# Attention and two MLPs on one core: the first MLP's last 1024 tokens in two blocks of 512

## The chip, the cores and the metric

The kernel runs on one core of a Trainium2 chip. The metric is the device time of one execution in microseconds (us): the median of the runs, with the lowest and the highest beside it.

## What is computed

Three stages follow one another: an attention over 4 batches of 8 heads with 576 tokens, a gated MLP on the 2304 tokens that come out of it, and a second MLP with two up projections. Cut to what matters here:

```python
x = attention(q, k, v, tau)          # 2304 tokens x 512
h = x @ w_in                         # 512 -> 2048
y = (h * sigmoid(h)) @ w_out         # 2048 -> 512
a, b = y @ w_a, y @ w_b              # 512 -> 1536 each
out = (a * b) @ w_o2                 # 1536 -> 512
```

All inputs are float32. Each operand of the MLPs' matmuls is split into a high part in the reduced format float32r and a low part (the rest), and each product is made of three matmuls: high by high, low weight by high, high weight by low.

## The kernel before

**Tiling.** Tokens lie along the columns of the matmuls in the first MLP. It works in 9 blocks of 256 tokens (`TB`, index `j`). A block has 16 slices of 128 features (index `f`); a slice with its block is a unit. The up part of a unit (`mlp1_up`) is 12 matmuls, three for each of four pieces of x, and fills one PSUM bank, `hb` or, from the fifth block on for every second unit, `hc`. The gate follows: tanh on ScalarE (line 713), `(tanh + 1) * h` on VectorE (line 716), the cast to the high part `gh` on ScalarE (line 719), the low part `gl` on VectorE (line 722). The down part (`mlp1_down`) is 12 matmuls of 256 columns that add the slice to y, which lies in two banks: `sb`, or `sd` for every second block after attention. On TensorE the up part of a unit stands ahead of the down part of the unit before it. At a block's end y is halved into `yo` by ScalarE and VectorE and stored to DRAM. x comes from DRAM as well, is cast on ScalarE (line 676) and subtracted on GpSimd (line 679).

The second MLP works in blocks of 512 tokens and 12 slices of 128 features. `mlp2_up` makes a and b (12 matmuls each, line 833), `mlp2_down` four groups of three matmuls (line 877), one for each 128 tokens, in four banks. Its input is loaded from DRAM and split by `load_y` (cast on line 807, subtraction on line 810).

**Weights.** Each of the 32 weight tiles of the first MLP and the 36 of the second is loaded as raw words and rebuilt in several steps (`split_weight`): `wt` on ScalarE (line 314), three VectorE operations (lines 321 to 330), a sum on GpSimd (line 334), the cast of the high part on ScalarE (line 338), and the low part on GpSimd or VectorE (line 342). The second MLP's weights take the places of the first's (ring `w`, 32) as its last block gives them up; the first four have places of their own (ring `w2`) from the end of attention on.

**Order.** Nothing is scheduled by the compiler. The class `Plan` lists tasks with an engine, a cost, a rank and the tasks they come after, and it holds rings: a taker of a ring waits until the one that many places before it has been freed. `run` plays the tasks through in modelled time, and this order is the order of the instructions on every engine and of the transfers on SP's queue. Each engine runs its instructions in that order. `closed` marks the end of attention, when its memory is given to others, and `closed1` the end of the first MLP.

Of the kernel before, what the change touches and what calls it, by code (L numbers as in the profile page):

```python
# [12 lines left out]
F32 = mybir.dt.float32  # L13
# [8 lines left out]
P = 128  # L22
# [10 lines left out]
NB = NT // TB  # L33
# [173 lines left out]
def fused_kernel(ctx: ExitStack, tc: tile.TileContext, qk, qk2, v, tau, w_in, w_out, w_a, w_b, w_o2, out):  # L207
# [19 lines left out]
    def pool(stack, name, bufs, side="left", **kw):  # L227
# [4 lines left out]
    p1, att = ExitStack(), ExitStack()  # L232
# [17 lines left out]
    ps_1 = pool(p1, "ps_1", 1, space=PSUM)  # L250
    ap = {n: pool(att, n, RINGS[n]) for n in ("qk", "v", "t", "e", "pa", "pb")}
# [206 lines left out]
    def softmax(parts, total):  # L458
# [10 lines left out]
        def scores():  # L469
            s["s"] = (ps_1 if bank == "sb" else ps_s).tile([P, 2, 512], F32, name=bank)  # L470
# [189 lines left out]
    up_last, down_last, y_dma = [None], [None], []  # L660

    def load_x(j):
        s = xs[j] = {}

        def split(c):
            need = [t for (b, half, heads), ts in x_dma.items() for t in ts
                    if heads == c and b * S + HALVES[half][0] < (j + 1) * TB and b * S + sum(HALVES[half]) > j * TB]

            def load():
                s["r", c] = xb_p.tile([P, TB], F32, name="xr", bufs=RINGS["xr"])  # L670
                nc.sync.dma_start(out=s["r", c], in_=xT_d[c, :, j * TB:(j + 1) * TB])

            def hi():
                s["h", c] = xb_p.tile([P, TB], F32R, name="xh")
                s["l", c] = xb_p.tile([P, TB], F32R, name="xl")
                nc.scalar.copy(out=s["h", c], in_=s["r", c])
# [4 lines left out]
            ld = dma(-1, P * 4 * TB, load, after=need, take=["xr"], slack=SLACK)  # L681
            h = pl.add("ACT", act_ns(TB), R_AUX, hi, [ld], ["xb"])
            l = pl.add("Pool", pool_ns(TB), R_AUX, lo, [h])
            pl.free("xr", l)
# [5 lines left out]
    def mlp1_up(n, j, f):  # L690
# [3 lines left out]
        bank = "hc" if n >= TWO_H and n % 2 else "hb"  # L694

        def up(c):
            def fn():
                if c == 0:
                    s["h"] = (pools["hc"] if bank == "hc" else ps_1).tile([P, 512], F32, name=bank)[:, :TB]
# [25 lines left out]
        for c in range(NC):  # L725
            p = pl.add("PE", 3 * pe_ns(TB), R, up(c),
# [4 lines left out]
            if f == NF - 1:  # L731
                pl.free("xb", p)
        th = pl.add("ACT", act_ns(TB, True), R_AUX, tanh, [p], ["g", "th"])
        ga = pl.add("DVE", dve_ns(TB), R_AUX, gate, [th])
        pl.free(bank, ga)
        hh = pl.add("ACT", act_ns(TB), R_AUX, hi, [ga])
        ll = pl.add("DVE", dve_ns(TB), R_AUX, lo, [hh], port=True)
        pl.free("th", ll)
        g_ready[j, f] = (hh, ll)

    def mlp1_down(n, j, f):


        ring = "sd" if j * NF >= TWO_H and j % 2 == 0 else "sb"
        prods = [(e, a, "gh") for e in range(NC) for a in (1, 0)] + [(e, 0, "gl") for e in range(NC)]

        def down(k0):
            def fn():
                if f == 0 and k0 == 0:
                    ys[j] = (pools["hc"] if ring == "sd" else ps_1).tile([P, 2, 512], F32, name=ring).rearrange("p k (e t) -> p (k e) t", e=2)  # L750
# [9 lines left out]
        for k0 in (0, 4, 8):  # L760
            p = pl.add("PE", 4 * pe_ns(TB), R, down(k0), [g_ready[j, f][k0 == 8], *w_ready["out", f]],
                       [ring] if f == 0 and k0 == 0 else [], behind=[down_last[0]])
# [243 lines left out]
```

## Time and profile before

| what | value |
|---|---|
| median of 3 runs | 1191.71 us |
| lowest and highest | 1190.04 and 1193.56 us |
| the profiled execution's own time | 1190.77 us |
| its span | 1189.0 us |
| TensorE's matmuls busy | 1154.5 us (97%) |
| weight loads on TensorE, beside them | 994.4 us (84%) |
| VectorE, ScalarE, GpSimd busy | 646.2, 543.9, 255.2 us |

A profile is of one execution. A busy time is what an engine's instructions took, one after another; matmuls overlap, so their single durations are longer than the distance from one to the next, and the distance is what a stream of them costs. An idle time before an instruction is given to the one that ended it. A wait for a transfer counts from the engine's side. Names such as `hb<-xh,w` mean that the tile `hb` is written from `xh` and `w`.

### The profile page before, as it was taken

The numbers are of one execution on the slowest core, as the hardware profiler recorded it, in microseconds if no ns is written. First come the engines' busy times: TensorE is split into PE (matmuls) and PEld (weight loads), VectorE is DVE, ScalarE is ACT, GpSimd is POOL, SyncE is SP. The second block draws the span as 40 slices with busy tenths as digits, with TensorE's granted clock in tenths as the row PEclk, the third lists the DMA queues.
The fourth block names the chain that finished last, engine by engine and source line by source line (L and its number), as shares of the span: only waits on it lengthen the run. The fifth ranks groups of instructions, "written<-read, shape, count | busy, mean of one in ns | idle before, by whom it ended". The sixth has DMA issues, their size and how long they took to land.

```text
span 1189.0 us, 19705 instructions
## 1 busy us (share of the span) xinstructions
PE 1154.5 (97%) x7675; PEld 994.4 (84%) x7675; DVE 646.2 (54%) x1448; ACT 543.9 (46%) x1071; POOL 255.2 (21%) x212
## 2 busy tenths in 40 slices
PE   8879999999999999989999999999999999999998
PEld 6556667898898888989999999877888888888898
DVE  7989897777777877473233257775211311211121
ACT  7777786666666766553233245443211211211121
POOL 3655554222111311131000034553000000000000
PEclk9999999999999999999999999999999999999999
DMA  5654543222322320261010024441100200000010
GB/s 192 197 175 144 168 155 132 77 85 81 100 74 71 108 73 33 67 191 54 1 37 28 1 72 143 127 139 56 69 1 1 71 1 1 18 36 1 1 36 18
DMA packets 43277, 90.15 MB, mean 76 GB/s; under 512 B 4384, under 2 KB 22448, under 8 KB 43184
## 3 DMA queue, kind: packets, MB, share of 16 engines
q1 hardware_dynamic: 43040, 88.89, 23.5%
q8 instruction: 60, 0.98, 0.3%
q14 instruction: 33, 0.27, 0.1%
q10 hardware_dynamic: 144, 0.00, 0.0%
HBM read 74.65 MB, written 14.23 MB: 75 GB/s over the span
## 4 chain that ended last, share of the span: by engine, by line
PE 65%; DVE 5%; DMA 3%; POOL 2%; issue 2%; ACT 1%; SPq 0%; POOLq 0%; DVEq 0%; ACTq 0%
PE op L877 11%; PE ps_b L833 11%; PE ps_a L833 10%; PE hb L704 8%; PE sb L754 7%; PE sd L754 4%; PE hc L704 4%; PE av L586 3%; PE sa L476 3%; PE tp L541 3%; POOL wt L334 2%; DVE wc L330 1%; DMA wraw<-w_a 1%; DVE wraw L325 1%; DVE wc L321 1%
## 5 line engine op out<-in xcount | busy, mean ns | idle before, releaser
L704 PE MATMUL hb<-xh,w 128*128 128x256 f32 x832 | 164.3, 291 | 3.1 <-DVE th L716 1.4
L843 DVE TENSOR_TENSOR z<-ps_b,z 128x512 f32<-128x512 f32 (+1 forms) x60 | 38.2, 637 | 230.8 <-PE ps_b L833 230.8
L833 PE MATMUL ps_a<-yh,w 128*128 128x512 f32 (+1 forms) x480 | 137.1, 370 | 0.3 <-POOL w L342 0.3
L833 PE MATMUL ps_b<-yh,w 128*128 128x512 f32 (+1 forms) x480 | 136.7, 369 | 0.4 <-DVE w L342 0.4
L704 PEld LDWEIGHTS hb<-xh,w 128*128 128x128 f32 x832 | 128.9, 191 | 9.1 <-issue 4.3
L877 PE MATMUL op<-w,zh 128*128 128x512 f32 x432 | 134.3, 392 | 0.0
L492 DVE TENSOR_SCALAR_CACHE_REDUCE t<-sa,nscale 128x576 f32<-128x576 f32 x128 | 103.5, 808 | 48.9 <-PE sa L476 47.6
L509 DVE SCALAR_TENSOR_TENSOR e<-t,thr,e 128x576 f32<-128x576 f32 x128 | 114.1, 891 | 16.7 <-ACT e L506 15.3
L704 PE MATMUL hb<-xl,w 128*128 128x256 f32 x416 | 117.5, 283 | 0.0
L334 POOL TENSOR_TENSOR wt<-wc,wt 128x512 uint32<-128x512 uint32 x68 | 91.9, 1351 | 114.2 <-DVE wc L330 93.4
L754 PE MATMUL sb<-gh,w 128*128 128x256 f32 x768 | 115.9, 286 | 0.0
L541 PE MATMUL tp<-ident,e 128*128 128x128 f32 x706 | 104.7, 277 | 10.6 <-DVE e L509 7.4
L506 ACT ACTIVATE e<-t,min 128x576 f32<-128x576 f32 x128 | 99.8, 782 | 25.4 <-DVE t L492 24.7
L840 ACT COPY z<-ps_a 128x512 f32<-128x512 f32 (+1 forms) x60 | 32.6, 543 | 163.1 <-PE ps_a L833 163.1
L541 PEld LDWEIGHTS tp<-ident,e 128*128 128x128 f32 x706 | 78.8, 140 | 32.4 <-DVE e L509 12.3
L754 PEld LDWEIGHTS sb<-gh,w 128*128 128x128 f32 x768 | 101.1, 191 | 3.3 <-issue 2.8
L833 PEld LDWEIGHTS ps_a<-yh,w 128*128 128x128 f32 x480 | 87.4, 188 | 17.3 <-POOL w L342 0.7
L833 PEld LDWEIGHTS ps_b<-yh,w 128*128 128x128 f32 x480 | 86.7, 188 | 16.2 <-DVE w L342 0.9
L877 PEld LDWEIGHTS op<-w,zh 128*128 128x128 f32 x432 | 80.3, 188 | 16.9
L846 ACT CAST zh<-z 128x512 fp32r<-128x512 f32 (+1 forms) x60 | 34.6, 577 | 128.3 <-DVE z L843 128.3
L722 DVE TENSOR_TENSOR gl<-th,gh 128x256 fp32r<-128x256 f32 x144 | 72.7, 505 | 33.9 <-ACT gh L719 33.6
L833 PE MATMUL ps_a<-yl,w 128*128 128x512 f32 (+1 forms) x240 | 88.9, 370 | 0.0
(97 smaller groups left out, 2173.3 us busy)
## 6 DMA issues: line engine op xcount, KB each, us to landing
qk<-qk SPq DMA_DIRECT2D x20, 576.0 KB
wraw<-w_in SPq DMA_DIRECT2D x16, 512.0 KB
wraw<-w_out SPq DMA_DIRECT2D x16, 512.0 KB
v<-v SPq DMA_DIRECT2D x20, 320.0 KB
wraw<-w_a SPq DMA_DIRECT2D x12, 512.0 KB
wraw<-w_b SPq DMA_DIRECT2D x12, 512.0 KB
wraw<-w_o SPq DMA_DIRECT2D x12, 512.0 KB
xr<-xT_d SPq DMA_DIRECT2D x36, 128.0 KB
```

The source lines that it names most:

```text
L334: nc.gpsimd.tensor_tensor(out=s["t"], in0=s["c"].bitcast(U32), in1=s["t"], op=ALU.add)
L476: nc.tensor.matmul(s["s"][:r + m, j, :NH], lhsT=hd["t"][:, 0, c - r:c + m], rhs=hd["t"][:, k, j * NH:(j + 1) * NH], start=(k == 1), stop=( ...
L492: nc.vector.tensor_scalar(out=s["t"], in0=s["s"][:, :, :NH], scalar1=nscale, scalar2=None, op0=ALU.mult, op1=ALU.min, accum_out=s["min"])
L506: nc.scalar.activation(out=s["e"], in_=s["t"], func=AF.Exp, scale=-1.0, bias=s["min"])
L509: nc.vector.scalar_tensor_tensor(out=s["e"], in0=s["s"][:, :, :NH] if early else s["t"], scalar=s["thr"], in1=s["e"], op0=ALU.is_ge if ear ...
L541: nc.tensor.transpose(t["tp"][:, j * P:(j + 1) * P], e["e"][:, o:o + P], ident)
L704: nc.tensor.matmul(s["h"], lhsT=w[:, a, o:o + P], rhs=xx, start=(c == 0 and k == 0), stop=(c == NC - 1 and k == 2))
L722: nc.vector.tensor_sub(out=s["gl"], in0=s["t"], in1=s["gh"].bitcast(F32))
L754: nc.tensor.matmul(ys[j][:, e, :], lhsT=w[:, a, e * P:(e + 1) * P], rhs=gs[j, f][g], start=(f == 0 and e % 2 == 0 and a == 1), stop=(f == ...
L833: nc.tensor.matmul(s[nm][:, :tn], lhsT=w[:, a, o:o + P], rhs=yy[:, :tn], start=(c == 0 and k == 0), stop=(c == NC - 1 and k == 2))
L843: nc.vector.tensor_mul(out=s["z"][:, :tn], in0=s["b"][:, :tn], in1=s["z"][:, :tn])
L877: nc.tensor.matmul(o_ps[t0, i], lhsT=s[z][:, i * P:(i + 1) * P], rhs=wt["o2", f][:, a, :], start=(f == 0 and k == 0), stop=(f == NF2 - 1 a ...
```

## The change

The blocks of the first MLP are listed in a table: five of 256 tokens and two of 512. In a wide block every matmul, gate operation, split of x and store has 512 columns, and y has one bank for each of its four pieces of 128 features. The table of banks in `mlp1_down` gives the fifth block (j = 4) `yc` and `yd`, the first wide block `ye`, `yf` and the two of `sb`, the last block `yc`, `yd`, `ye` and `yf`. `sb` moves to a pool of its own, and the second MLP's first two banks (`pools["ab", 0]`) are opened over it when the first wide block's y has left (`close_b`), not at the end of attention. Wide blocks have their own buffers in SBUF (`b5`), opened at the end of attention: five places for split pieces of x, two for raw ones.

In the second MLP the split y has two sets of four places in place of six in all; the second set is opened at the end of the first MLP. Raw y has one buffer in place of two. All of the first 32 weight tiles take places that the last block of the first MLP gives up, and the last four take `w2`, now opened at `closed1`.

```diff
-NB = NT // TB
+BLOCKS = tuple((i * TB, TB) for i in range(5)) + ((5 * TB, 512), (5 * TB + 512, 512))
...
-    RINGS = dict(qk=2, sp=2, v=1, t=2, e=4, pa=1, pb=1, sa=1, sb=1, tp=2, hb=1, hc=1, sd=1, av=1, x=1, xi=1, rs=1,
+    RINGS = dict(qk=2, sp=2, v=1, t=2, e=4, pa=1, pb=1, sa=1, sb=1, tp=2, hb=1, hc=1, yc=1, yd=1, ye=1, yf=1, xr5=2, x5=5, g5=2, th5=1, av=1, x=1, xi=1, rs=1,
...
-                 yr=2, y2=6, za=2, zb=2, z=2, ob=2, o0=1, o1=1, o2=1, o3=1)
+                 yr=1, y2a=4, y2b=4, za=2, zb=2, z=2, ob=2, o0=1, o1=1, o2=1, o3=1)
...
 def load_x(j):
+        t0, tn = BLOCKS[j]
+        big = tn > TB
+        ring, raw = ("x5", "xr5") if big else ("xb", "xr")
...
-            ld = dma(-1, P * 4 * TB, load, after=need, take=["xr"], slack=SLACK)
+            ld = dma(-1, P * 4 * tn, load, after=need, take=[raw], slack=SLACK, behind=[closed] if big else [])
...
 def mlp1_down(n, j, f):
-        ring = "sd" if j * NF >= TWO_H and j % 2 == 0 else "sb"
+        banks = {4: ("yc", "yd"), 5: ("ye", "yf", "sb"), 6: ("yc", "yd", "ye", "yf")}.get(j, ("sb",))
+        per = T2 // tn
...
-                    nc.tensor.matmul(ys[j][:, e, :], lhsT=w[:, a, e * P:(e + 1) * P], rhs=gs[j, f][g],
-                                     start=(f == 0 and e % 2 == 0 and a == 1), stop=(f == NF - 1 and g == "gl"),
+                    nc.tensor.matmul(ys[j][e // per][:, e % per * tn:(e % per + 1) * tn], lhsT=w[:, a, e * P:(e + 1) * P], rhs=gs[j, f][g],
+                                     start=(f == 0 and e % per == 0 and a == 1), stop=(f == NF - 1 and g == "gl"),
...
+            outs = ("yo", "yo", "th5", "xr5") if last else ("yo",) * NC
...
 def load_y(t0):
+        ab = "ab"[t0 // T2 % 2]
...
-            h = pl.add("ACT", act_ns(tn), R_AUX, hi, [ld], ["y2"])
+            h = pl.add("ACT", act_ns(tn), R_AUX, hi, [ld], ["y2" + ab], behind=[closed1] if ab == "b" else [])
...
 def close_attention():
-        pools["w2"] = pool(ctx, "wpool2", RINGS["w2"], "right")
-        pools["y"] = pool(ctx, "yb", 6, "right")
+        pools["ya"] = pool(ctx, "ya", 4, "right")
+        pools["b5"] = pool(p1, "b5", 1)
         pools["hc"] = pool(p1, "ps_hc", 1, space=PSUM)
+        pools["y5"] = pool(p1, "ps_y5", 1, space=PSUM)
+
+    def close_b():
+        psb.close()
         pools["ab", 0] = pool(ctx, "ps_ab", 1, "right", space=PSUM)
...
 def close_mlp1():
+        pools["w2"] = pool(ctx, "wpool2", RINGS["w2"])
+        pools["yb"] = pool(ctx, "ybb", 4)
...
-        split_weight(key, src, 1e6 + i, "w2" if i < RINGS["w2"] else "w", [closed], ("Pool", "DVE")[i % 2])
+        split_weight(key, src, 1e6 + i, *(("w", [closed]) if i < 32 else ("w2", [closed1])), ("Pool", "DVE")[i % 2])
```

**TensorE, where the first wide block begins.** Of the kernel before, the up part of a unit on `hc` and the down part of the unit before it, near the end of the first MLP (the other units read the same):

```order
L704 MATMUL hc_9607<-xh_8455,w_1926 128x256 x2
L704 MATMUL hc_9607<-xl_8456,w_1926 128x256
L704 MATMUL hc_9607<-xh_8461,w_1983 128x256 x2
L704 MATMUL hc_9607<-xl_8462,w_1983 128x256
L704 MATMUL hc_9607<-xh_8528,w_2063 128x256 x2
L704 MATMUL hc_9607<-xl_8529,w_2063 128x256
L704 MATMUL hc_9607<-xh_8542,w_2135 128x256 x2
L704 MATMUL hc_9607<-xl_8543,w_2135 128x256
L754 MATMUL sd_9070<-gh_9597,w_2333 128x256 x8
L754 MATMUL sd_9070<-gl_9598,w_2333 128x256 x4
```

Of the change, the end of the wide block's first up part, the last down part of the narrow block before it, and the beginning of the next up part (lines 713 and 773 are the lines 704 and 754 of before):

```order
L713 MATMUL hb_7341<-xh5_6969,w_452 128x512 x2
L713 MATMUL hb_7341<-xl5_6970,w_452 128x512
L773 MATMUL yc_6797<-gh_7328,w_2415 128x256 x4
L773 MATMUL yd_6798<-gh_7328,w_2415 128x256 x4
L773 MATMUL yc_6797<-gl_7329,w_2415 128x256 x2
L773 MATMUL yd_6798<-gl_7329,w_2415 128x256 x2
L713 MATMUL hc_7372<-xh5_6831,w_244 128x512 x2
L713 MATMUL hc_7372<-xl5_6832,w_244 128x512
```

The matmuls of a unit stay 12 up and 12 down with twice the columns, and the order of up and down parts is the same.

**ScalarE, after the end of attention.** Before, from the eviction of the fourth block's y on (`wt<-wraw` is the first step of a weight of the second MLP, `th` a tanh, `gh` its cast):

```order
L771 ACTIVATE yo_6799<-sb_5556 128x512
L676 CAST xh_6807<-xr_6714 128x256
L807 CAST yh_6820<-yr_6770 128x512
L713 ACTIVATE th_6830<-hc_6786 128x256
L807 CAST yh_6835<-yr_6777 128x512
L719 CAST gh_6831<-th_6830 128x256
L314 ACTIVATE wt_6865<-wraw_6784 128x512
L713 ACTIVATE th_6873<-hb_6845 128x256
L719 CAST gh_6874<-th_6873 128x256
L314 ACTIVATE wt_6889<-wraw_6791 128x512
```

Of the change, from the same eviction on:

```order
L793 ACTIVATE yo_6780<-sb_5555 128x512
L723 ACTIVATE th_6803<-hc_6773 128x256
L729 CAST gh_6804<-th_6803 128x256
L833 CAST yha_6822<-yr_6771 128x512
L682 CAST xh5_6831<-xr5_6757 128x512
L682 CAST xh5_6842<-xr5_6764 128x512
L723 ACTIVATE th_6854<-hb_6817 128x256
L316 ACTIVATE wt_6858<-wraw_6778 128x512
L729 CAST gh_6855<-th_6854 128x256
L316 ACTIVATE wt_6877<-wraw_6787 128x512
```

The first weight split stood ahead of a unit's tanh and now stands between its tanh and its cast; two wide casts of x have come ahead of that tanh.

**TensorE, from the first MLP to the second.** Before, the last two down parts (`sd`) and the first matmuls of the second MLP:

```order
L754 MATMUL sd_9070<-gh_9597,w_2333 128x256 x8
L754 MATMUL sd_9070<-gl_9598,w_2333 128x256 x4
L833 MATMUL ps_a_9646<-yh_6820,w_6918 128x512 x2
L833 MATMUL ps_a_9646<-yl_6821,w_6918 128x512
L754 MATMUL sd_9070<-gh_9632,w_2412 128x256 x8
L754 MATMUL sd_9070<-gl_9633,w_2412 128x256 x4
L833 MATMUL ps_a_9646<-yh_6835,w_7049 128x512 x2
```

Of the change, from the end of the down part of the 15th slice on (line 859 is the line 833 of before):

```order
L773 MATMUL ye_7932<-gl5_8550,w_2336 128x512
L773 MATMUL yf_7933<-gl5_8550,w_2336 128x512
L773 MATMUL yc_7930<-gh5_8597,w_2415 128x512 x2
L773 MATMUL yd_7931<-gh5_8597,w_2415 128x512 x2
L773 MATMUL ye_7932<-gh5_8597,w_2415 128x512 x2
L773 MATMUL yf_7933<-gh5_8597,w_2415 128x512 x2
L773 MATMUL yc_7930<-gl5_8598,w_2415 128x512
L773 MATMUL yd_7931<-gl5_8598,w_2415 128x512
L773 MATMUL ye_7932<-gl5_8598,w_2415 128x512
L773 MATMUL yf_7933<-gl5_8598,w_2415 128x512
L859 MATMUL ps_a_8638<-yha_6822,w_8000 128x512 x2
```

The last two down parts now follow each other without the three matmuls of the second MLP between them.

## Rows read from the trace of the kernel before

**Rows 1.** Busy time of each engine by stretch (x instructions), TensorE's granted clock, DMA.

```profile
core 0: us, PE busy (x) PEld busy (x) DVE busy (x) ACT busy (x) POOL busy (x), PEclk, DMA share, GB/s
...
500.00:550.00 50.00, 46.34 (x375) 45.08 (x375) 32.02 (x61) 23.27 (x53) 14.13 (x13) 1.00 0.48 147
550.00:691.00 141.00, 141.00 (x1178) 141.00 (x1177) 43.51 (x101) 43.43 (x112) 7.32 (x10) 1.00 0.07 22
691.00:735.00 44.00, 43.69 (x365) 43.49 (x364) 32.13 (x60) 23.87 (x52) 18.59 (x14) 1.00 0.34 109
735.00:830.00 95.00, 94.26 (x417) 76.82 (x416) 64.09 (x98) 40.79 (x68) 44.17 (x33) 1.00 0.37 117
830.00:1131.00 301.00, 301.00 (x1313) 246.08 (x1312) 63.06 (x94) 54.33 (x93) 0.00 (x0) 1.00 0.06 20
```

**Rows 2.** The chain that ended last: start us, us, engine, tile, line, count.

```profile
559.02 1.44 PE hc L704 x12
...
812.30 2.75 PE ps_b L833 x12
```

**Rows 3.** TensorE's timeline in the second MLP's last block: start us, us, operation.

```profile
1131.81 0.40 PE L833 MATMUL ps_a<-yh,w 128*128 128x256 f32 x2
...
1133.23 0.40 PE L833 MATMUL ps_b<-yh,w 128*128 128x256 f32 x2
```

**Rows 4.** TensorE's waits from 500 to 830 us: total us, times, longest.

```profile
PE sd L754 <- ACT gh L719: 3.1, 5, 1.7
PE sd L754 <- DVE gl L722: 0.9, 2, 0.7
PE ps_b L833 <- DVE w L342: 0.4, 1, 0.4
PE ps_a L833 <- POOL w L342: 0.3, 1, 0.3
```

**Rows 5.** Timeline of one unit's gate in an undisturbed stretch, idle before in brackets.

```profile
580.34 0.28 PE L704 MATMUL hb<-xl,w 128*128 128x256 f32 x1
580.66 0.38 ACT L713 ACTIVATE th<-hb 128x256 f32<-128x256 f32 x1 [1.60 <-PE hb L704]
581.08 0.42 DVE L716 SCALAR_TENSOR_TENSOR th<-th,hb 128x256 f32<-128x256 f32 x1 [1.56 <-ACT th L713]
581.53 0.41 ACT L719 CAST gh<-th 128x256 fp32r<-128x256 f32 x1 [0.49 <-DVE th L716]
...
583.34 1.12 PE L754 MATMUL sb<-gh,w 128*128 128x256 f32 x8
```

**Rows 6.** Groups by shape, the second MLP's: count, busy us, mean ns, idle before.

```profile
L843 DVE TENSOR_TENSOR z<-ps_b,z 128x512 f32<-128x512 f32 x48 | 33.1, 690 | 196.9 <-PE ps_b L833 196.9
...
L846 ACT CAST zh<-z 128x512 fp32r<-128x512 f32 x48 | 29.8, 620 | 110.6 <-DVE z L843 110.6
L840 ACT COPY z<-ps_a 128x512 f32<-128x512 f32 x48 | 28.1, 585 | 138.8 <-PE ps_a L833 138.8
```

**Rows 7.** Timeline after the end of attention: a weight's issue, ScalarE, TensorE.

```profile
501.80 0.42 SPq L310 DMA_DIRECT2D wraw<-w_a  x1
...
508.89 0.67 ACT L314 ACTIVATE wt<-wraw 128x512 uint32<-128x512 uint32 x1 [3.16 <-DMA wraw<-w_a]
...
509.46 0.37 ACT L713 ACTIVATE th<-hb 128x256 f32<-128x256 f32 x1
...
510.31 0.41 ACT L719 CAST gh<-th 128x256 fp32r<-128x256 f32 x1 [0.49 <-DVE th L716]
...
510.77 1.22 PE L754 MATMUL sd<-gh,w 128*128 128x256 f32 x8 [1.68 <-ACT gh L719]
```

**Rows 8.** Line 338 from 690 to 850 us (ns min/median/max, starts), and TensorE's wait.

```profile
L338 ACT CAST w<-wt x32: 616/622/624, 697.0 to 820.4; 128x512 fp32r<-128x512 f32 x32
...
802.38 0.73 PE L833 MATMUL ps_a<-yh,w 128*128 128x512 f32 x2 [0.30 <-POOL w L342]
```

More of the change, by code (lines that the diff above doesn't have):

```diff
@@ L469, in scores @@
         def scores():
[L470 removed]
+            s["s"] = (ps_b if bank == "sb" else ps_s).tile([P, 2, 512], F32, name=bank)
             if parts[0][0]["split"]:
@@ L694, in mlp1_up @@
         bank = "hc" if n >= TWO_H and n % 2 else "hb"
+        tn = BLOCKS[j][1]
+        big = tn > TB
+        ring, part, xring = ("g5", "th5", "x5") if big else ("g", "th", "xb")
         def up(c):
@@ L760, in mlp1_down @@
         for k0 in (0, 4, 8):
-            p = pl.add("PE", 4 * pe_ns(TB), R, down(k0), [g_ready[j, f][k0 == 8], *w_ready["out", f]],
-                       [ring] if f == 0 and k0 == 0 else [], behind=[down_last[0]])
+            p = pl.add("PE", 4 * pe_ns(tn), R, down(k0), [g_ready[j, f][k0 == 8], *w_ready["out", f]],
+                       banks if f == 0 and k0 == 0 else [], behind=[down_last[0], *([closed] if j >= 4 and f == 0 else [])])
             down_last[0] = p
         w_last["out", f] = p
-        pl.free("g", p)
+        pl.free("g5" if big else "g", p)
@@ L780, in mlp1_down @@
             evs = []
-            for k in range(2):
-                ev = pl.add(("ACT", "DVE")[k], (act_ns, dve_ns)[k](2 * TB), -2, halve(k), [p], ["yo"])
+            for k in range(NC // per):
+                ev = pl.add(("ACT", "DVE")[k % 2], (act_ns, dve_ns)[k % 2](T2), -2, halve(k), [p], [outs[k]])
                 evs.append(ev)
-                st = dma(-1, 2 * P * 4 * TB, store(k), after=[ev])
-                pl.free("yo", st)
-                y_dma.append(st)
-            pl.free(ring, *evs)
+                st = dma(-1, P * 4 * T2, store(k), after=[ev])
+                pl.free(outs[k], st)
+                y_dma.append((t0, tn, st))
@@ L790, in fused_kernel @@
+            for i, bk in enumerate(banks):
+                pl.free(bk, *(evs[i:] if bk == "sb" else evs[i:i + 1]))
+            if j == 5:
+                b_done.extend(evs[2:])
     y2, y2_ready, zs, z_ready, o_ps = {}, {}, {}, {}, {}
@@ L793, in load_y @@
         tn = min(T2, NT - t0)
-        need = y_dma[2 * (t0 // TB):2 * ((t0 + tn) // TB)]
+        need = [t for a, m, t in y_dma if a < t0 + tn and a + m > t0]
+        ab = "ab"[t0 // T2 % 2]
         def split(c):
@@ L854, in mlp2_up @@
                 p = pl.add("PE", 3 * pe_ns(tn), 1e5 + 2 * n, up(nm, c), [*y2_ready[t0, c], *w_ready[nm, c, f // 4]],
-                           ["z" + nm] if c == 0 else [], behind=[up_last[0], *([closed1] if n % 2 and c == 0 else [])])
+                           ["z" + nm] if c == 0 else [], behind=[up_last[0], *([closed1 if n % 2 else closed_b] if c == 0 else [])])
                 up_last[0] = p
                 if nm == "b" and f == NF2 - 1:
-                    pl.free("y2", p)
+                    pl.free("y2" + "ab"[t0 // T2 % 2], p)
             last[nm] = p
@@ L945, in close_mlp1 @@
         pools["ab", 1] = pool(ctx, "ps_ab2", 1, space=PSUM)
-    closed1 = pl.add("none", 1, 0, close_mlp1, behind=[up_last[0], down_last[0], closed, *y_dma])
+        pools["w2"] = pool(ctx, "wpool2", RINGS["w2"])
+        pools["yb"] = pool(ctx, "ybb", 4)
+    closed_b = pl.add("none", 1, 0, close_b, behind=[closed, *b_done])
+    closed1 = pl.add("none", 1, 0, close_mlp1, behind=[up_last[0], down_last[0], closed, closed_b, *(t for *_, t in y_dma)])
     for i in range(36):
```

76 lines of the change are left out of this document (44 added, 32 removed).

## The prediction

> **What bounds the kernel now.** I read the busy times by stage first: they say in which stage TensorE ever stops. Then the chain of waits, for the pitch of TensorE's matmuls; then TensorE's own waits, and the timeline around each of them; last the durations by shape of the engines that feed it.
>
> [Rows 1] The reader is to see that from 550 to 691 us and from 830 to 1131 us TensorE's busy time equals the stretch, at a granted clock of 1.00 (2.4 GHz), while VectorE, ScalarE and GpSimd are busy for a third of it or less. In those stretches nothing but the number and the pitch of matmuls counts. The two stretches differ in width: 1178 matmuls of 256 columns take 141 us, that is 119.7 ns each; 1313 matmuls, of 512 columns all, take 301 us, 229.2 ns each. [Rows 2] The chain of waits shows the same pitch, twelve narrow ones in 1.44 us and twelve wide ones in 2.75 us. [Rows 3] That it is the width and not the line is seen in the last block of the second MLP, where line 833, wide elsewhere, runs at 256 columns: twelve from 1131.81 to 1133.23 us, 118 ns each.
>
> Up to the end of attention the built order on TensorE is the same before and after, so I leave that stage out. After it, TensorE stops for 3.66 us in the stretch from 500 to 550, 0.31 from 691 to 735 and 0.74 from 735 to 830 [rows 1]. [Rows 4] All of it has an owner: the split g (ScalarE's and VectorE's half) is late for the down matmuls, and twice a weight tile of the second MLP is.
>
> **The wide matmuls.** Four blocks of 256 tokens have 16 feature slices each, with 12 up and 12 down matmuls: 4 x 16 x 24 = 1536 narrow ones, which become 768 wide ones with the same columns in all. Two narrow cost 239.4 ns, one wide 229.2: 10.2 ns less, times 768 is **7.8 us**, all of it on the path, since TensorE bounds the stage. The built order lists 512 columns in both blocks, on up and down, so the change does what it says.
> A rule stands against the size of this. The Trainium skill, "TensorE: Matmul & The Clock Gate", section "Back-to-back issue gap", gives an isolated matmul N/2.4 + 2.5 ns, 109.2 and 215.8: by that a pair saves 2.6 ns, the 768 save an estimated 2.0 us, and the whole sum below would be 4.2 us and not 10.0. The trace does not agree with either figure (119.7 and 229.2), so I take its rows.
>
> **Work on the other engines.** Per unit of columns ScalarE, VectorE and GpSimd get fewer and longer instructions (64 tanh, gate, cast and subtraction sets become 32; 16 splits of x become 8, evictions of y stay 18). I cost it at nothing: TensorE covers it. The cover is the slack of the chain up, tanh, gate, cast, down. [Rows 5] Now the last up matmul ends at 580.46, the cast at 581.94, the down matmul starts at 583.34: 1.4 us to spare in a pitch of 2.88 us. The operations sum to 1.21 us, the hand-overs to 0.27. [Rows 6] Wide ones are bounded by the same forms in the second MLP: 0.585 + 0.690 + 0.620 + 0.27 = 2.17 us, in 2 x 2.75 us: 3.3 us to spare. If weight splitting used all that up, each unit would wait for the rest of it.
>
> **The stall after attention.** [Rows 7] It is a queue effect: ScalarE stands at the first weight split until that weight has landed (issued at 501.80, used at 508.89), the tanh of a unit is behind it, and TensorE waits 1.68 us. The rest of the 3.66 us follows while ScalarE and VectorE prepare the four early weights and split y. In the new order only two weights start there and stop half way, so the later part should go. The first part does not: now the tanh stands ahead of the weight split but its cast stands behind it, and on SP two x loads of 256 KB go ahead of the weight. If it lands 1 us later for them (my guess), the cast ends near 511.0 (509.9 + 0.67 + 0.41), for a down matmul that was due at 509.1 (510.77 less 1.68). I take 2.0 us; bounds 0.5 (all but a short wait goes) and 5 (3.7 and another late landing). Gain **1.7**, from -1.3 to 3.2.
>
> **Weights of the second MLP.** [Rows 8] A weight's cast of its high half on ScalarE marks its progress: 32 of them start from 697.0 to 820.4 us, 3.98 us apart. By 735 us ten have started, with the four early ones 14; the 25th is needed at the ninth slice, at 802.38, and TensorE waits there for it and for its neighbour, 0.3 + 0.4 us [rows 4]. Now none is prepared early, and the first place is free only when the fourth slice of the last block is through its up part, some 17 us into it (3 x 5.5). But that block lasts 16 x 5.5 = 88 us in place of 46: 71 us for 18 weights at the old pace, and 66 us more to the ninth slice. The 0.74 us go: **0.7**, bounds 0 and 0.7. The 0.31 us before the boundary comes from the same work with 1.4 us of slack and should go with 3.3: **0.3**.
>
> **The end of the first MLP.** The last up part is followed by the down part of the slice before, 2.75 us, and then at once by its own; three matmuls of the second MLP that stood between are gone. Against 2.17 us that leaves 0.6, and ahead of the tanh in ScalarE's queue is a weight split of 0.67 us which waits for GpSimd. I take a loss of **0.5**, bounds 0 and 2 (two such operations late).
> The second set of y buffers takes waits from a stage, 830 to 1131 us, in which TensorE has none [rows 1]: nothing. The one y buffer for landing makes SP hold each y load until the last one is split; at the start of the second MLP SP holds weights behind it, and ScalarE's copy of a behind a split of y. That copy is needed 11 us later by the first down part; it is covered unless a load takes over 5 us. Four banks of y are taken anew for the first wide block, freed ones for the second: up to one unit lies between, 2.75 us, against one eviction of 0.69.
>
> **Sum.** 7.8 + 1.7 + 0.7 + 0.3 - 0.5 = 10.0 us against the profiled execution's 1190.8: 1180.8. The median of the runs shown is 0.9 above that execution and the lowest 0.7 below; I give back 0.4 for it: **1181.2 us**. With the good ends, 7.8 + 3.2 + 0.7 + 0.3 = 12.0: 1179; with the bad, 7.8 - 1.3 - 2 = 4.5: 1186.7.
>
> **The rivals.**
> *Most of the width's gain is not there.* The pitch at 512 columns was measured in the second MLP, and in the first a wide matmul may cost twice the 118.3 ns of the narrow ones of line 833 [rows 3], because its y goes round four banks: 2.8 ns a pair, 2.2 us, and 4.4 with the other terms: 1186.8. For: nothing in the rows but that 118.3 is below 119.7. Against: line 877, within the stretch from 830 to 1131 us, goes round four banks at full pitch [rows 1]. Chance 0.05. The Trainium skill's formula above comes to nearly the same time, an estimated 1187.
> *The edges take it back.* In-order ScalarE waits for a load (x, y or weight) at the three edges: after attention, between the two wide blocks (where three of four x pieces are split only as the old ones come free), and at the second MLP's start. Two or three further waits, each of 1.7 us as now after attention up to 3 us, give 1185 to 1190. For: the order puts such splits ahead of tanh at each. Against: 3.3 us of slack. Chance 0.13.
> *The weights come too late.* Now it ends slower. The place is the ninth slice of the second MLP's first block. The 25th weight has 71 + 66 = 137 us, 5.5 us each; from there each further 0.1 us costs 2.5 us, and with a pace of 6.2 in place of 3.98 TensorE waits 18 us: 1199. For it: each weight passes ScalarE twice, behind wide tanh and cast. Against: the built order has 19 casts within the last block, so the pace would have to fall after that. Chance 0.04.
> *The clock.* The wide down parts change banks at every one or two matmuls, and TensorE could fall to 1.2 GHz in them: the 32 units' 384 down matmuls (384 x 229.2 ns = 88 us) would take up to double, up to 1269. Against: from 830 to 1131 us line 877 changes banks at every third matmul, at 1.00 [rows 1]. Chance 0.01. The Trainium skill, "TensorE: Matmul & The Clock Gate", section "A second HAM failure mode: psum-queue depth-cycling", tells of such a loss at 512 columns; no row here shows it.
>
> **How the numbers follow.** A measurement of this kernel can tell about 0.3%, 3.6 us, from no change. Forecast 0.75 (1179 to 1184.5), narrow gain 0.05, edges 0.13, weights 0.04, clock 0.01; 0.02 for what I did not see. Faster: 0.75, the 0.05 at 1186.8, and 0.07 of the edges, 0.87; within: the rest of the edges and 0.02, 0.08; slower 0.05. The range from 1177.5 to 1187.5 holds the forecast with its bounds, the narrow gain and half of the edges: some 0.86.
>
> **What would show it.** Right: wide up and down matmuls twelve in 2.75 us; no idle of TensorE inside the wide blocks; waits for g only within 25 us of attention's end and at the last slice; no wait for a second-MLP weight; the second MLP starting about 9 us earlier. Wrong: twelve wide ones in over 2.8 us; a wait for x at the second wide block's start; a wait for w at any slice of the second MLP; a granted clock below 1.00 after 500 us.

## The result, and the profile after

The changed kernel takes **1181.24 us**, median of 4 runs (1177.8 to 1183.84), the kernel before 1191.57 in the runs beside it (1190.04 to 1193.56): ratio 0.9907, 95% interval 0.989 to 0.9924, 10.3 us less. The forecast was 1181.2.

The profiled execution is the fastest of the four, 1177.8 us with a span of 1176.0 (before: 1189.0). Trace against trace the gain is therefore 13.0 us, 2.7 more than between the medians.

Busy time by stretch in the changed kernel (columns as in [rows 1]); the second MLP now starts at 726.96 us, before at 735.10:

```profile
500.00:550.00 50.00, 47.62 (x382) 46.52 (x381) 24.09 (x46) 18.89 (x44) 9.29 (x7) 1.00 0.39 118
550.00:722.00 172.00, 170.44 (x754) 140.23 (x752) 81.55 (x122) 61.92 (x104) 36.51 (x28) 1.00 0.19 60
...
727.00:821.00 94.00, 94.00 (x410) 76.76 (x409) 55.71 (x87) 36.31 (x62) 32.71 (x25) 1.00 0.34 107
821.00:1118.00 297.00, 297.00 (x1305) 244.80 (x1304) 61.24 (x91) 52.79 (x90) 0.00 (x0) 1.00 0.06 19
```

TensorE still waits five times: twice after attention, and three times in the last 26 us of the first MLP. From 727 us on the trace lists no wait; the 0.74 us for weights in [rows 4] are gone. TensorE's waits from 490 us on in sum, and the five in its timeline:

```profile
PE yc L773 <- ACT gh L729: 5.6, 5, 2.0
```

```profile
509.78 0.74 PE L773 MATMUL yc<-gh,w 128*128 128x256 f32 x4 [1.98 <-ACT gh L729]
519.08 0.74 PE L773 MATMUL yc<-gh,w 128*128 128x256 f32 x4 [0.37 <-ACT gh L729]
...
701.73 0.73 PE L773 MATMUL yc<-gh,w 128*128 128x512 f32 x2 [0.54 <-ACT gh L729]
719.26 0.73 PE L773 MATMUL yc<-gh,w 128*128 128x512 f32 x2 [0.91 <-ACT gh L729]
724.07 0.74 PE L773 MATMUL yc<-gh,w 128*128 128x512 f32 x2 [1.80 <-ACT gh L729]
```

Before, the waits were 4.7 us in all [rows 4]; now they are 5.6, in other places. After attention 3.66 us became 2.35; at the end of the first MLP 0.31 became 3.25. ScalarE's timeline says why. First after attention, then before the last down part:

```profile
506.18 0.62 ACT L833 CAST yha<-yr 128x512 fp32r<-128x512 f32 x1 [2.82 <-DMA yr<-yT_d]
506.71 1.14 ACT L682 CAST xh<-xr 128x512 fp32r<-128x512 f32 x2
507.75 0.38 ACT L723 ACTIVATE th<-hb 128x256 f32<-128x256 f32 x1
...
509.33 0.41 ACT L729 CAST gh<-th 128x256 fp32r<-128x256 f32 x1 [0.65 <-DVE th L726]
```

```profile
721.49 0.67 ACT L316 ACTIVATE wt<-wraw 128x512 uint32<-128x512 uint32 x1 [1.54 <-DMA wraw<-w_b]
722.07 0.58 ACT L723 ACTIVATE th<-hc 128x512 f32<-128x512 f32 x1
723.40 0.62 ACT L729 CAST gh<-th 128x512 fp32r<-128x512 f32 x1 [0.75 <-DVE th L726]
```

In both, ScalarE stands at work for the second MLP whose transfer has not landed (a piece of y; a weight), and the tanh that TensorE needs next is behind it. The wait of 0.37 us has a piece of y ahead of it too (0.77 us, at 516.89). The two of 0.54 and 0.91 us are of another kind. Before the first of them:

```profile
698.75 1.68 DVE L332 SCALAR_TENSOR_TENSOR wc<-wc,wraw 128x512 uint32<-128x512 uint32 x1
...
701.06 0.62 ACT L729 CAST gh<-th 128x512 fp32r<-128x512 f32 x1 [0.20 <-DVE th L726]
```

The cast starts when VectorE's gate ends, and the gate stands behind a step of a weight that takes 1.68 us here and 0.69 at 695.66. Ahead of that the tanh stood behind a cast of a weight (line 340) that waited 1.53 us for GpSimd. It is the same before the second (1.67 and 1.58 us). Why the weight's step is long there was not followed.

The surprise is the pitch. TensorE's timeline in two blocks of the second MLP, start and duration; from one first row of twelve matmuls to the next is the time of those twelve:

```profile
773.86 0.63 PE L859 MATMUL ps_a<-yha,w 128*128 128x512 f32 x2
...
776.62 0.62 PE L859 MATMUL ps_b<-yha,w 128*128 128x512 f32 x2
...
779.37 0.63 PE L903 MATMUL op<-w,zh 128*128 128x512 f32 x2
...
782.14 0.63 PE L859 MATMUL ps_a<-yha,w 128*128 128x512 f32 x2
...
831.70 0.61 PE L859 MATMUL ps_a<-yhb,w 128*128 128x512 f32 x2
...
834.42 0.61 PE L859 MATMUL ps_b<-yhb,w 128*128 128x512 f32 x2
...
837.14 0.61 PE L903 MATMUL op<-w,zh 128*128 128x512 f32 x2
...
839.86 0.61 PE L859 MATMUL ps_a<-yhb,w 128*128 128x512 f32 x2
```

A block that reads set a (yha) takes 2.76, 2.75 and 2.77 us for twelve, much as the kernel before did [rows 2]. A block that reads set b (yhb) takes 2.72 three times, 226.7 ns each. So do the wide blocks of the first MLP; an up part and the down part behind it:

```profile
599.99 0.61 PE L713 MATMUL hb<-xh,w 128*128 128x512 f32 x2
...
602.71 0.61 PE L773 MATMUL ye<-gh,w 128*128 128x512 f32 x2
...
605.42 0.61 PE L713 MATMUL hc<-xh,w 128*128 128x512 f32 x2
```

Even `op`, which reads no y, changes with the block. It switches at the first ps_a of each block (823.54, 921.46 us).

The 13.0 us between the traces, in order of time: 1.3 in attention, whose order did not change; 1.3 after it (3.66 to 2.35); 768 x (239.4 - 226.7) ns = 9.75 by the wide matmuls; -2.9 at the end of the first MLP (0.31 to 3.25); 0.74 for weights; and the second MLP's rest, 2.8. This last is worked out so: from its first matmul to the end of the span it takes 1176.0 - 726.96 = 449.0 us, before 1189.0 - 735.10 less the 1.43 of first-MLP matmuls within it, 452.5; of the 3.5, 0.74 are the waits.

### The profile page after: what moved, and what is told of

Read it like the earlier page. It is cut to its first block, busy times and chain, and to the rows that moved or that the text cites. A ratio compares the mean times of both kernels' runs of the same rounds, so it can differ in the third digit from the quotient of the medians.

```text
span 1176.0 us, 17925 instructions
## 1 busy us (share of the span) xinstructions
PE 1140.8 (97%) x6907; PEld 953.9 (81%) x6907; DVE 636.6 (54%) x1384; ACT 530.1 (45%) x999; POOL 250.8 (21%) x204
## 4 chain that ended last, share of the span: by engine, by line
PE 76%; DVE 8%; DMA 8%; ACT 3%; issue 3%; POOL 2%; SPq 0%; DVEq 0%; POOLq 0%; ACTq 0%
PE ps_a L859 13%; PE op L903 13%; PE ps_b L859 13%; PE hb L713 9%; PE sb L773 7%; PE av L588 5%; PE tp L543 5%; PE sa L478 4%; PE hc L713 3%; DMA xi<-r_d 2%; DVE wraw L327 2%; DVE wc L332 1%; DMA wraw<-w_a 1%; PE yf L773 1%; PE ye L773 1%
## 5 line engine op out<-in xcount | busy, mean ns | idle before, releaser
L713 PE MATMUL hb<-xh,w 128*128 128x256 f32 (+1 forms) x704 | 156.2, 312 | 3.1 <-POOL w L344 1.5
L713 PE MATMUL hb<-xl,w 128*128 128x256 f32 (+1 forms) x352 | 106.2, 302 | 0.0
L773 PE MATMUL sb<-gh,w 128*128 128x256 f32 (+1 forms) x576 | 97.0, 299 | 0.0
L773 PEld LDWEIGHTS sb<-gh,w 128*128 128x128 f32 x576 | 80.1, 190 | 5.7 <-issue 2.8
L903 PE MATMUL op<-w,zl 128*128 128x512 f32 x216 | 84.6, 391 | 0.0
L344 POOL TENSOR_TENSOR w<-wt,w 128x512 fp32r<-128x512 f32 x50 | 67.8, 1356 | 56.1 <-ACT w L340 56.0
L732 DVE TENSOR_TENSOR gl<-th,gh 128x256 fp32r<-128x256 f32 (+1 forms) x112 | 65.6, 586 | 25.0 <-ACT gh L729 24.8
L859 PE MATMUL ps_a<-yha,w 128*128 128x512 f32 (+1 forms) x288 | 77.3, 355 | 0.0
L859 PE MATMUL ps_b<-yha,w 128*128 128x512 f32 (+1 forms) x288 | 77.0, 354 | 0.0
L478 PE MATMUL sa<-sp 128*128 128x288 f32 (+1 forms) x400 | 69.6, 300 | 1.1 <-DVE t L494 1.1
```

The source lines that it names most:

```text
L344: eng.tensor_tensor(out=wt[key][:, 1, :], in0=s["t"].bitcast(F32), in1=wt[key][:, 0, :].bitcast(F32), op=ALU.subtract)
L478: nc.tensor.matmul(s["s"][:r + m, j, :NH], lhsT=hd["t"][:, 0, c - r:c + m], rhs=hd["t"][:, k, j * NH:(j + 1) * NH], start=(k == 1), stop=( ...
L713: nc.tensor.matmul(s["h"], lhsT=w[:, a, o:o + P], rhs=xx, start=(c == 0 and k == 0), stop=(c == NC - 1 and k == 2))
L732: nc.vector.tensor_sub(out=s["gl"], in0=s["t"], in1=s["gh"].bitcast(F32))
L773: nc.tensor.matmul(ys[j][e // per][:, e % per * tn:(e % per + 1) * tn], lhsT=w[:, a, e * P:(e + 1) * P], rhs=gs[j, f][g], start=(f == 0 an ...
L859: nc.tensor.matmul(s[nm][:, :tn], lhsT=w[:, a, o:o + P], rhs=yy[:, :tn], start=(c == 0 and k == 0), stop=(c == NC - 1 and k == 2))
```

## The experiments

Two theories stood against each other: that the width makes the gain, and that the banks, the weights' place or the two y sets make it. Besides, the late waits and the two pitches were open. Times are medians, with the ratio to the kernel before beside it.

**1. Nine narrow blocks, the rest of the change kept.**

```diff
-BLOCKS = tuple((i * TB, TB) for i in range(5)) + ((5 * TB, 512), (5 * TB + 512, 512))
+BLOCKS = tuple((i * TB, TB) for i in range(9))
-        banks = {4: ("yc", "yd"), 5: ("ye", "yf", "sb"), 6: ("yc", "yd", "ye", "yf")}.get(j, ("sb",))
+        banks = {4: ("yc", "yd"), 5: ("ye", "yf"), 7: ("yc", "yd"), 8: ("ye", "yf")}.get(j, ("sb",))
```

> All nine blocks of 256 tokens; the banks of y for each 128 features stay for blocks 4, 5, 7 and 8 (as pairs), so do the two sets of y buffers and the ring of 32 weights. Theory (the width is the gain): 768 wide matmuls become 1536 narrow ones; by the pitches of the changed kernel's trace, 2 x 119.7 against 226.7 ns, that is 9.8 us more, less what goes of the 3.25 us of late stalls (0.54, 0.91, 1.80): 1188 to 1191 us, beside the kernel before. Rival (the gain comes from the banks, the y sets or the place of the weights): under 1185 us.

Measured: 1204.48 us, ratio 1.0112 (1.0093 to 1.0131). More than either theory: slower than the kernel before. TensorE's largest wait from 490 us on, and two stretches with its granted clock:

```profile
PE ps_a L859 <- POOL w L344: 12.9, 4, 5.8
```

```profile
805.00:815.00 10.00, 3.82 (x13) 2.25 (x11) 5.63 (x11) 3.21 (x5) 5.15 (x4) 0.77 0.51 136
815.00:850.00 35.00, 30.44 (x123) 24.75 (x124) 19.00 (x30) 12.79 (x21) 11.70 (x9) 0.87 0.24 74
```

This is the prediction's rival "the weights come too late", in a kernel where it does decide. The second MLP's first 32 weights now all wait for places that the first MLP's last block gives up, and a narrow last block gives them up within half the time. In the ten us in which TensorE is busy for 3.8, its granted clock is 0.77, in the next 35 us 0.87: part of the time the lower of its two levels (1.2 and 2.4 GHz) was granted. So the width is also what lets the weights share one pool; the run did not isolate what that is worth.

**2. Narrow, with the first four weights in a pool of their own, as before.** To run 1:

```diff
+        pools["w2"] = pool(ctx, "wpool2", RINGS["w2"], "right")
         pools["ya"] = pool(ctx, "ya", 4, "right")
...
-*(("w", [closed]) if i < 32 else ("w2", [closed1]))
+*(("w2", [closed]) if i < 4 else ("w", [closed]))
```

> Nine blocks of 256 as in the narrow run, but the second MLP's weights where they were before: the first four in a pool of their own, opened at the end of the attention. So against the kernel before it has the banks of y per 128 features and the two y sets, and not the width; its weights are no longer late. Theory (the narrow run's 1204 us were 14 us of late weights and the clock drop behind them; the width is worth 9.8 us of pitch, less the changed kernel's 5.6 us of stalls; the banks and the sets are worth what is left): 1185 to 1188 us, no wait at ps_a or ps_b over 1.5 us. Rival 1 (the width alone makes the gain of the change, banks and sets nothing): 1190 to 1193 us, as before. Rival 2 (late weights are not the cause of the 1204 us): over 1195 us.

Measured: 1195.61 us, ratio 1.0024 (1.0011 to 1.0037). The waits of ps_a for weights fall from 12.9 us to 0.8 and the time by 8.9: the late weights are indeed most of what the 1204 us are above the kernel before, though the time lies by 0.6 us within rival 2's range. But the theory's 1185 to 1188 was wrong too: the banks and the two sets with narrow blocks gain nothing and cost 0.24%. The four largest waits:

```profile
PE op L903 <- ACT zh L872: 2.4, 2, 2.1
PE yc L773 <- ACT gh L729: 1.5, 2, 1.3
PE ps_b L859 <- DVE w L344: 1.1, 1, 1.1
PE ps_a L859 <- POOL w L344: 0.8, 2, 0.6
```

By these rows the second MLP waits 4.3 us where the kernel before waited 0.7. Why zh was late by 2.1 us was not followed. What follows: without the width there is no gain.

**3. One ring of six y buffers**, four where set a lies and two where set b lies.

```diff
-        ab = "ab"[t0 // T2 % 2]
+            i = (NC * (t0 // T2) + c) % 6
+            ab = "a" if i < 4 else "b"
```

> One ring of six y buffers as before in place of two sets of four; four of the six lie where set a lies, two where set b lies, so that a block mixes both. Theory (the second set is worth nothing): 1181 us, within 0.2% of the changed kernel. Rival (the buffers of set b make the matmuls of their blocks faster, 226.7 against 230 ns): the time goes up by part of 2.7 us, and in the trace the matmuls of one block that read the two buffers of set b stand at 2.72 us for 12, those that read set a at 2.76. If instead whole blocks keep one pitch, whatever buffers they read, the buffer isn't the cause.

Measured: 1185.42 us, ratio 0.9953 (0.9937 to 0.9969): 4.2 us more than the changed kernel, and the intervals of the two don't meet. So the second set is not worth nothing. No wait was added: TensorE's only waits after 490 us are for gh, 5.7 us. All groups of twelve in the second MLP's wide blocks take 2.74 to 2.78 us, and it takes 1183.6 - 731.05 = 452.5 us as in the kernel before. The price is in the pitch, and two of six buffers at set b's place do not bring it back. By the expectation's last sentence the buffer would then not be the cause; runs 4 and 5 show that this was the wrong test, because a group of twelve also slows down with its neighbours.

**4. A ring of seven at set b's place for all blocks but the first.**

```diff
-        ab = "ab"[t0 // T2 % 2]
+        ab = "ab"[t0 > 0]
-        pools["yb"] = pool(ctx, "ybb", 4)
+        pools["yb"] = pool(ctx, "ybb", 7)
```

> The first block of the second MLP reads set a; all later ones read a ring of seven buffers where set b lies (in the changed kernel the blocks alternate a, b, a, b, a). Theory (the place of the y buffers sets the pitch of the whole block): second, third and fourth block all at 2.72 us for 12 matmuls, 1.5 us less, 1179.8 us. Rival 1 (it is each second block, whatever it reads): the third block stays at 2.76, time as of the changed kernel, 1181.2 us. Rival 2 (two blocks that share a ring, whose buffers shift from block to block, are both slow, as in the run with the ring of six): 2.74 to 2.78 everywhere, 1184 to 1185 us.

Measured: 1181.77 us, ratio 0.9904 (0.9872 to 0.9936). In the trace the second, third and fourth block all stand at 2.72 us, the first at 2.75 to 2.77: the pitch goes with where y lies, neither with the ring nor with each second block. The median does not show the 1.5 us; the interval is over twice as wide as that on either side.

**5. 64 unused bytes.** By the compiled program's list of buffers, everything on the left side of SBUF that TensorE reads in the MLPs (weights, x, g, z, set b) starts at 32 modulo 128, and everything on the right side (set a; in the kernel before all of y and four weights) at 96. The next kernels only shift a side.

```diff
+    pad_r = pool(ctx, "pad_r", 1, "right").tile([P, 16], F32, name="pad_r")
+    nc.vector.memset(pad_r, 0.0)
```

> The changed kernel with 64 bytes of unused memory at the right end of SBUF, so that the buffers on the right side (set a, the raw weights and their helpers) lie at addresses of 32 modulo 128, as all on the left side do (the weights, set b), where they lay at 96. Nothing else moves, no instruction changes. Theory (the pitch of a block hangs on how the address of y lies against that of the weights, modulo 128): the first and third block of the second MLP go from 2.76 to 2.72 us for 12 matmuls as well, 1.5 us each, 1178.2 us. Rival (it is the region, the upper end of SBUF, or the side): they stay at 2.76, 1181.2 us.

> The changed kernel with 96 unused bytes at the left end and 224 at the right, so that every buffer that TensorE reads in the two MLPs lies at 0 modulo 256; no instruction changes. Theory 1 (only the difference between the two sides matters): the same as with the shift of 64 bytes, 2.72 us for 12 in all wide blocks, 1178.2 us. Theory 2 (a row that starts at a multiple of 128 is read in one line less, whatever the other operand): shorter still, under 2.70 us for 12, and the narrow steps under 1.43, some 5 us or more in all, 1175 us or less. Rival (neither: the region or the side): 1181.2 us.

> The changed kernel with 64 unused bytes at the left end, so that every buffer that TensorE reads in the MLPs, on both sides, lies at 96 modulo 128. Theory 1 (what counts is that weights and moving operand lie alike): 2.72 us for 12 in all wide blocks as with the shift of the right side, about 1179.5 us. Theory 2 (an operand at 96 is itself slower to read): all wide blocks at 2.74 to 2.79, in the first MLP too, where 768 matmuls at 3.5 ns more and half of the second MLP's give some 5 us more, 1185 us or above.

In the second of these the pads are 96 bytes on the left and 224 on the right; in the third 64 on the left and none on the right. Measured: 1179.5 us, ratio 0.9894 (0.9873 to 0.9916); 1180.43, 0.9894 (0.9878 to 0.9911); 1181.27, 0.9902 (0.9878 to 0.9926). The timeline of the first of them, in the block that reads set a:

```profile
780.85 0.62 PE L861 MATMUL ps_a<-yha,w 128*128 128x512 f32 x2
...
783.57 0.62 PE L861 MATMUL ps_b<-yha,w 128*128 128x512 f32 x2
...
786.28 0.62 PE L905 MATMUL op<-w,zh 128*128 128x512 f32 x2
...
789.00 0.62 PE L861 MATMUL ps_a<-yha,w 128*128 128x512 f32 x2
```

2.72, 2.71 and 2.72 us, where it was 2.76, 2.75 and 2.77. All three kernels have 2.71 to 2.73 in every wide block of the second MLP, but for a single 2.74, with both sides at 32, at 0 and at 96. So no address is good or bad by itself: a block runs at 2.72 when all that TensorE reads in it starts alike modulo 128. Theory 2 falls in both expectations, and so does the region.

That each matmul goes by its own two operands is not shown, and the kernel before speaks against it. Its four early weights are those of a and b for the first two of the four pieces of y, in the first four slices; they start at 96 as y does. In such a slice:

```profile
834.21 0.62 PE L833 MATMUL ps_a<-yh,w 128*128 128x512 f32 x2
...
835.60 0.62 PE L833 MATMUL ps_a<-yh,w 128*128 128x512 f32 x2
...
836.97 0.62 PE L833 MATMUL ps_b<-yh,w 128*128 128x512 f32 x2
```

The first six matmuls, whose operands lie alike, take 1.39 us, the six behind them, 64 apart, 1.37; at 2.72 for twelve it would be 1.36. In run 2, where by the same list those four weights start at 96 again, a and b of the first four slices take 2.79 each in the blocks that read set b; those of the other eight slices take 2.72.

In the traces of the three kernels the second MLP takes 446.8, 446.7 and 446.8 us against 449.0. The medians move by 1.7, 0.8 and 0 us, but each interval overlaps that of the changed kernel (0.989 to 0.9924), because the stages ahead vary more: the times alone do not show this gain, the pitch does. The second MLP's start in the profiles of kernels with the same order lies between 726.96 and 734.61 us.

**6. The same 64 bytes in the kernel before.**

> The kernel before, with the 64 unused bytes at the right end alone: its one ring of y and its first four weights of the second MLP, at 96 modulo 128 so far, lie at 32 as all other operands do. Theory (the second part of the change gained only by the address of set b): the second MLP, 452.5 us from the first ps_a to the end in the kernel before (453.9 less the 12 first-MLP matmuls inside it), comes to about 447.4, so 5.1 us less in all, about 1187 us, ratio 0.9957; 12 matmuls of ps_a, ps_b and op at 2.72 us in all wide blocks. Rival (the two sets gain something else, which no address gives): under 2 us, ratio over 0.998.

Measured in five rounds: 1188.76 us, ratio 0.9974 (0.9965 to 0.9983), 3.6 us less. Smaller than the 5.1 expected and more than the rival's 2. In the trace the second MLP takes 1188.7 - 738.65 - 1.43 = 448.6 us against 452.5; its waits for weights are 1.2 us where they were 0.7. Away from waits and from the change of width, the twelve stand at 2.72:

```profile
861.62 0.62 PE L835 MATMUL ps_a<-yh,w 128*128 128x512 f32 x2
...
864.34 0.62 PE L835 MATMUL ps_b<-yh,w 128*128 128x512 f32 x2
...
867.06 0.62 PE L879 MATMUL op<-w,zh 128*128 128x512 f32 x2
...
869.78 0.62 PE L835 MATMUL ps_a<-yh,w 128*128 128x512 f32 x2
```

In the last block, of 256 columns, the shift does the opposite. Twelve of line 835 there:

```profile
1142.21 0.40 PE L835 MATMUL ps_b<-yh,w 128*128 128x256 f32 x2
...
1143.65 0.63 PE L879 MATMUL op<-w,zh 128*128 128x512 f32 x2
```

That is 1.44 us for ps_b and 1.43 for ps_a, where the kernel before has 1.39 to 1.42 for both (1.42 for the first ps_a, [rows 3]): 0.6 us more over the block. With 0.5 us more of waits that is about what is missing between the 447.4 us expected for the second MLP and the 448.6 measured.

The run also separates the width from the pitch of the second MLP. With both kernels shifted, 1188.76 and 1179.5 us, the ratios (each to the kernel before in its own rounds) 0.9974 and 0.9894, the rest of the change is worth 0.8%, some 9 us.

**7. The waits.** First the y loads and weights of the second MLP only behind the third unit of the first wide block; then the planner told that weights land 2 us later.

```diff
+            if (j, f, c) == (5, 2, 0):
+                late[0] = p
-            ld = dma(-1, P * 4 * tn, load, after=[*need, closed], take=["yr"])
+            ld = dma(-1, P * 4 * tn, load, after=[*need, closed], take=["yr"], behind=[late[0]])
-*(("w", [closed]) if i < 32 else ("w2", [closed1]))
+*(("w", [closed, late[0]]) if i < 32 else ("w2", [closed1]))
```

```diff
-        a = dma(rank, P * 4096, load, take=["wraw"], behind=after)
+        a = dma(rank, P * 4096, load, take=["wraw"], behind=after, slack=2000)
```

(The slack is for the second MLP's weights alone.)

> The loads of y for the second MLP and all its weights may start only behind the third unit of the first wide block (in the changed kernel the first of them are issued at the end of the attention). Theory (the 2.35 us of stalls after the attention come from ScalarE, which stands in order behind y and weight transfers that are not needed before 727 us): 1178.8 us, no TensorE wait over 0.5 us between 500 and 530 us. Rival (the x transfer or the gate chain is late next): under 1 us gained, 1180.5 us or more.

> The planner is told that the second MLP's weights land 2 us later, so it places ScalarE's first step on each further back; nothing else. Theory (the late stalls of 0.54, 0.91 and 1.80 us come from ScalarE waiting for a weight transfer in front of the tanh or cast that TensorE needs): 1178 us, and no TensorE wait over 0.3 us between 690 and 727 us. Rival (the weights are then late for the second MLP, or the wait is the gate chain's own): 1181 us or more, with a wait at a ps_a or ps_b instead.

Measured: 1177.64 us, ratio 0.9886 (0.9868 to 0.9903), and 1179.18, 0.9893 (0.9875 to 0.9912). With the later loads TensorE is busy for 50.00 of the 50 us from 500 to 550; the three waits at the end stay and grow, from 3.25 us to 3.89:

```profile
702.09 0.73 PE L776 MATMUL yc<-gh,w 128*128 128x512 f32 x2 [0.82 <-ACT gh L730]
719.83 0.73 PE L776 MATMUL yc<-gh,w 128*128 128x512 f32 x2 [1.13 <-ACT gh L730]
724.79 0.73 PE L776 MATMUL yc<-gh,w 128*128 128x512 f32 x2 [1.94 <-ACT gh L730]
```

With the slack it is the other way round, and only partly:

```profile
519.52 0.74 PE L773 MATMUL yc<-gh,w 128*128 128x256 f32 x4 [1.54 <-ACT gh L729]
...
718.98 0.73 PE L773 MATMUL yc<-gh,w 128*128 128x512 f32 x2 [0.36 <-ACT gh L729]
722.96 0.74 PE L773 MATMUL yc<-gh,w 128*128 128x512 f32 x2 [0.96 <-ACT gh L729]
```

The end's 3.25 us became 1.32, not under 0.3 each as expected: the cast of gh now waits 1.5 to 2.1 us for VectorE's gate (698.58 to 701.29 us), which stands in VectorE's order behind weight work, as it did in the changed kernel before its waits of 0.54 and 0.91. Both intervals overlap that of the changed kernel (0.989 to 0.9924), so what each edit removes is read from the waits and not from the medians.

**8. All of it, and with the 64 bytes.** The two edits of 7, the ring of 4, and the second MLP's first ps_a ahead of the last down step:

```diff
+    a0["up"]["first"].append(a0["down"])
+    a0["down"]["wait"] += 1
```

> The late y and weight loads, the planner's 2 us, the ring of seven, and the second MLP's first 12 matmuls of ps_a put ahead of the last down step of the first MLP, where TensorE waited 1.8 us. Theory (the parts add up: 2.3 us after the attention, 1.9 at the end of the first MLP, 1.3 more by the cover, 1.5 by the pitch if the place of the buffers sets it): 1174.3 us, all TensorE waits between 490 and 740 us under 1.5 us in sum. Rival (they take the same time twice, or a new wait comes, of ps_a for its weights): 1177 us or more, not better than the better of the two single runs.

> The run with all the later loads, the ring of seven and the first ps_a ahead of the last down step, with the 64 bytes added. Theory (the shift adds to it, as one block of the second MLP is left at 2.76): 1.5 us less than that run, 1174 us against 1192.5 of the kernel before, ratio about 0.9847. Rival (the run's waits grow as TensorE gets faster, or the shift does nothing here): as that run, ratio 0.986 or more.

Measured: 1175.65 us, ratio 0.986 (0.9831 to 0.9889); with the shift **1173.55 us**, ratio 0.9845 (0.9831 to 0.9859). The parts add up within 1.4 us. The interval of the first includes the ratio of the second, so the shift's 1.5 us is not shown by this pair of times. That last kernel has the lowest median: 18.8 us under the kernel before in the same rounds, 7.7 under the changed one, measured in others. All the waits that its trace lists for TensorE from 490 us on:

```profile
PE op L912 <- DVE zl L882: 0.6, 1, 0.6
PE op L912 <- ACT zh L879: 0.4, 1, 0.4
PE yc L778 <- ACT gh L732: 0.3, 1, 0.3
```

The list is not all that it loses: between 756 and 790 us seven groups of twelve take 2.88 to 3.75 us, 3.0 us above 2.72 in sum, of which the list holds 1.0. They were not followed.

## Why the prediction was right, and where it wasn't

The main mechanism was right: fewer and wider matmuls, in a stage that TensorE bounds. That the total was right to 0.1 us is luck: two terms were mis-sized and one was put at nothing, they cancel, and the four runs of the changed kernel lie between 1177.8 and 1183.84.

- **Wide matmuls, 7.8 us: mis-sized, 9.75.** The step took the second MLP's 229.2 ns for a wide matmul [rows 1, 2]. That row was itself slowed, by the place of y; where all operands lie alike a wide one takes 226.7, in the first MLP's blocks as well. A pair saves 12.7 ns, not 10.2. The formula of the Trainium skill, "TensorE: Matmul & The Clock Gate", section "Back-to-back issue gap", which would have given an estimated 2.0 us, does not fit these rows: its 109.2 and 215.8 ns stand against 119.7 and 226.7.
- **Stall after attention, gain 1.7: came as 1.3** (3.66 to 2.35 us, 2.0 forecast). The place was right, the landing that ScalarE stood at was another: a piece of y both times (2.82 and 0.77 us), at which the step did not look. Run 7 shows that the stall goes whole when neither y nor weights stand there; it moved both together.
- **Weights, 0.74 us: right**, no wait after 727 us. The 0.31 us at the boundary went, but a larger wait took its place:
- **End of the first MLP, loss 0.5: mis-sized, 3.25 us.** The step bounded it at 2 for the last down part (1.80 there), but it named GpSimd's result as what ScalarE stands at; there it stands at the weight's landing. And it missed two waits before (0.54, 0.91), inside the last wide block, where its signs allowed none. In those ScalarE did stand at GpSimd's result, and VectorE's gate stood behind a long weight step: the "3.3 us of slack" was counted without weight work and transfers. The prediction said what weight splitting would do if it used the slack up, and gave it no price.
- **Two sets of y, nothing: wrong.** It reasoned about waits, of which there were none, and there it was right. That the second set's place would change the pitch of half the second MLP, 2.8 us in the trace, was not in any row of before; run 3 shows that it is lost with the set, runs 5 and 6 that the address does it, though not why.
- **Other engines' work, nothing:** right up to 690 us: TensorE is busy for 139.89 of the 140 us from 550. After that it is the loss above.

Sum of the forecast terms 10.0, of the measured ones 9.75 + 1.3 + 0.74 - 2.9 + 2.8 = 11.7 in one trace, with 1.3 more in attention that no part of the change explains; between medians 10.3.

Of the rivals, "the edges take it back" was partly true (5.6 us of waits: two after attention, as it named, three ahead of the second MLP, none between the wide blocks) and was paid for by the pitch. "The weights come too late" did not happen, but run 1 has its mechanism and a worse price, with the clock in it. "Most of the width's gain is not there" falls by the 2.72 us; its 118.3 ns came from a row with y 64 apart, where narrow matmuls take less and wide ones more (run 6). The clock stayed at 1.00 from 550 to 1118 us through all wide down parts, with a change of bank at every one or two matmuls. The loss that the Trainium skill describes in "TensorE: Matmul & The Clock Gate", section "A second HAM failure mode: psum-queue depth-cycling", was not seen here.

## What to carry to other kernels

Before a pitch from one stage is used to price another, ask whether the row is clean: twelve wide matmuls at 2.76 and at 2.72 us looked like one number and were two. When TensorE bounds a stage, look at where its operands start, modulo 128: 64 unused bytes were worth 0.26% of a kernel that was not otherwise touched. Judge such a change by whole blocks, as neighbours slow each other, and at each width by itself. And slack of an engine that works in order is not slack if a transfer stands ahead in its queue: count the landing and the other work of the engines in the chain, or move what is not needed yet.

## What the runs showed of the hardware

- For float32r matmuls of 512 columns with a weight load each, twelve take 2.71 to 2.73 us in a block where all that TensorE reads starts at the same address modulo 128 (0, 32 and 96 were tried). Where part of it lies 64 apart, a and b take 2.73 to 2.79 us for twelve, and nearly all slices of three such groups (a, b, `op`) 8.24 to 8.29 in place of 8.16: 1.0 to 1.6%.
- The loss belongs to the stretch and not to the single matmul: `op`, whose own operands lie alike, takes 2.77 us in blocks that read set a, and six matmuls of a that lie alike among others that don't take 1.39. A mechanism for this was not found. Whether differences of 32 or 96 cost the same wasn't tried.
- At 256 columns it is the other way round: in the second MLP's last block twelve take 1.43 to 1.44 us where all lies alike, and 1.39 to 1.42 where y lies 64 apart.
- Alignment to a multiple of 256 gains nothing beyond that: 2.72 us as at 32.
